# An RWKV-7 block and a SwiGLU block on one core: copies and scalings moved from VectorE to ScalarE, with a new order

## The chip, the cores and the metric

The kernel runs on one core of one Trainium2 chip. The time is the device time of one execution in microseconds (us), and the median of several runs counts. Each core has five engines that work side by side, each with its own queue that it takes in order: TensorE (PE in the profile, its weight loads PEld), VectorE (DVE), ScalarE (ACT), GpSimd (POOL) and SyncE (SP). SP and POOL here mostly issue DMA transfers.

## What is computed

Two blocks follow each other. The first is a recurrence over 768 time steps, for 4 batches of 8 heads with a head size of 40; its outputs are the tokens of the second, a feed-forward block over 3072 tokens of width 320 with 1536 hidden units.

```python
for t in range(S):
    y[:, :, t] = np.einsum('bhd,bhde->bhe', rt, state)
    Sa = np.einsum('bhde,bhe->bhd', state, at)
    state_decay = state * wt[:, :, None, :] - np.einsum('bhd,bhe->bhde', Sa, bt)
    state = state_decay + np.einsum('bhd,bhe->bhde', vt, kt)
...
rms = np.sqrt(np.mean(x * x, axis=-1, keepdims=True) + 1e-06)
xn = x / rms * rms_g
g = xn @ w_gate
silu = g * (1.0 / (1.0 + np.exp(-g)))
val = xn @ w_val
return (silu * val @ w_out).astype(np.float32)
```

The output at step t reads the state before that step's update, so the state that the last step leaves is read by nothing.

## The kernel before

The 768 steps are cut into 24 chunks of 32 (`NCH`, `C`). All 32 pairs of batch and head are worked on together: the 128 partitions hold two groups (`i`), two halves of the heads or of the factors (`o`, `q`), and the 32 steps of a chunk. All data is fp32.

Three stages make a chunk, and a fourth is shared by two chunks:

- `front(c)` loads w, a, k, b and v, transposes them on TensorE, and builds the products inside the chunk level by level (`LEVELS`: pairs of steps, then 4, 8, 16, 32). It leaves `LT`, the triangular matrices, `KN[l]`, the decayed k and b by level, with `KN[32]` for the whole chunk, `aP`, the decayed a, and `T[l]`, the products of the decays. `front` and `inverse` are written two chunks ahead of `main`.
- `inverse(c)` inverts the unit triangular matrices: 31 steps of two VectorE operations each (`tmp`, `Yi`), with transfers through DRAM (`sB`, `M`, `sY`) before and after to change the layout.
- `main(c)` is the recurrence proper. TensorE makes X from the incoming state and v, ScalarE negates it into `Xs`, TensorE makes U from it, and U is copied into `VU` beside v. From `VU` and `KN[32]` TensorE makes the state's update (kind `"update"`), and VectorE adds the decayed old state, `Sdec`, to it (`ST`). For the outputs, every second chunk loads and transposes the queries: `rE` holds them, and `r2` the same with the partition halves exchanged. Scores of queries against `VU` are masked into `As`, one part for each level, with the masks `msi`. The levels' products are summed into `y` (`down`). Last, tokens are transposed, normalized (`x`) and transposed again, and `xg` takes them times the norm's weights `gcol`, a column over partitions.
- `feed(g)` is the feed-forward block for the 256 tokens of two chunks. For each of 12 slices of 128 hidden units it loads weights (`wf`), makes gate and value products on TensorE (kinds `"h64"` and `"h"`), takes silu on ScalarE (`sg`), multiplies on VectorE (`hT`) and accumulates the output product in `po` (kind `"out"`). Before the first feed, `narrow` brings the float64 weights to fp32 and stores them in DRAM as `sW`; that is VectorE and ScalarE work (`ex`, `wf`, `o`).

Which engine does an operation is written in the helper's name: `tt`, `dcopy`, `ts` and `where` go to VectorE, `copy`, `act` and `scale` to ScalarE, `pe` to TensorE. `scale(o, a, by)` multiplies by a constant or by a column of one value for each partition.

The order of the work is written out by hand. Each helper call makes a piece in a list, with the pieces it depends on; `Plan.issue` then emits the pieces in the order of the string `ORDER`. A word of it says how far ahead of the first piece not yet emitted the next one stands; `-` emits a warm-up matmul into an unused part of `po` (L1000), which keeps TensorE busy in the first 230 us. `PAIRS` says which of three PSUM tiles each use of PSUM takes. Since all engines take their queues in order, this string fixes what stands before what on every engine. The functions that follow are the ones that the change touches; most profile lines name the helper (L475 VectorE, L502 and L505 ScalarE copies and scalings, L521 and L524 TensorE), so the tiles' names tell the operations apart.

Of the kernel before, what the change touches and what calls it, by code (L numbers as in the profile page):

```python
# [7 lines left out]
FP32 = mybir.dt.float32  # L8
# [8 lines left out]
P = 128  # L17
C = 32
LEVELS = (1, 2, 4, 8, 16)
CG = 2  # L20
WB = 5
S0, S1 = 15.0, 2.0
LEAD = 2
WARM = 230.0
# [21 lines left out]
36 33 2 26 42 1 31 0 25 343 37 29 107 38 24 36 26 34 262 2 13 1 35 40 0 190 24 339 13 14 - - - 40 17 44 15 41 43 55  # L46
42 8 60 47 175 72 48 45 84 185 59 68 186 585 54 58 - - - - - 49 93 586 53 179 69 71 599 81 176 57 597 50 67 178 609
70 188 80 622 51 92 16 623 65 610 52 56 177 633 64 66 - - - - - - - - - - - - 61 189 9 598 77 79 187 78 587 620 62 0
587 81 - - - - 72 75 179 82 62 90 595 384 194 588 87 11 633 89 589 74 395 620 197 590 380 88 73 195 391 - - - - 101
196 209 390 610 84 102 214 381 201 611 202 5 212 86 213 383 591 85 0 222 92 591 611 17 95 221 224 223 384 94 234 225  # L50
- - 197 233 237 93 391 245 246 592 328 393 198 598 645 612 0 641 598 15 612 592 - 338 205 206 380 642 599 209 0 207
612 200 0 337 612 186 598 6 326 613 2 599 641 34 176 200 216 217 23 600 389 215 33 201 355 95 202 177 96 214 - - - -
211 187 339 93 0 577 0 561 578 297 579 171 192 53 187 191 - - - 182 188 200 623 172 185 625 186 580 562 581 612 355
582 199 1065 197 583 611 183 198 624 184 0 152 1005 850 298 0 298 0 837 295 0 0 0 83 130 298 148 0 298 83 0 507 307
833 0 303 555 0 840 307 0 290 0 67 125 316 314 0 132 125 67 0 0 131 314 0 286 325 0 130 0 298 130 0 291 292 - - - -
- 287 0 293 0 304 0 316 305 301 0 0 283 0 296 0 311 0 322 281 0 286 0 295 280 0 292 - - - - - - - - - - - - - - - -
- 288 0 0 0 0 301 0 285 62 301 116 305 0 283 250 116 0 - - - - - - - - 293 0 258 112 296 0 110 300 256 0 308 307 245
293 292 0 0 304 0 288 0 301 - - - - - - 298 306 0 0 313 0 297 0 0 0 293 310 494 301 0 494 0 302 0 0 299 492 0 0 296
0 246 0 791 0 0 0 787 0 0 93 468 2 796 94 469 0 94 462 794 0 467 93 94 290 461 95 462 96 468 511 97 469 291 98 470
481 289 99 292 471 0 99 100 101 471 102 472 103 481 511 104 482 105 488 106 489 107 483 2 490 108 109 0 293 109 490  # L60
0 108 0 0 379 0 379 387 0 387 369 0 405 378 387 406 0 - - - - - - - - - - - - - - - - - - - - - - - - - - - - - - -
- - - - - - - - - - - - - - - - - - - - - - - - - - - - - - - - - - - - - - - - 44 0 367 377 0 415 0 42 0 414 383 43
412 0 383 410 0 383 40 373 0 0 0 0 0 0 36 0 377 - - - - - - - - - - - - - - - - - 44 0 377 35 44 0 414 0 0 82 0 32 -
43 0 373 0 90 0 229 407 38 88 0 40 78 226 42 38 41 47 48 0 43 226 42 50 45 48 396 0 50 396 43 0 396 0 0 379 395 380
0 395 380 0 401 0 394 0 378 242 400 44 0 400 47 0 145 45 377 242 0 145 391 377 0 216 1 145 391 42 635 398 429 626
146 0 397 39 145 426 634 398 146 147 631 43 623 44 621 45 632 46 148 47 622 - - - - 639 375 376 149 48 416 239 641
830 150 399 377 640 840 0 150 641 653 48 838 151 658 152 645 828 - - - - - - 642 153 670 154 646 155 682 49 656 50
156 669 657 51 157 666 158 667 52 159 643 668 - - - - - - - 53 389 160 161 678 162 1 651 652 - 647 2 702 655 3 654 0
594 610 611 609 625 595 636 109 608 110 596 373 - - - - - - - - - - - 605 590 374 111 345 783 607 626 782 383 112
627 620 622 385 793 113 623 606 375 382 114 792 621 - - - - - - - 617 384 115 376 346 116 377 619 117 635 634 118  # L70
618 378 119 - - - - - 160 633 120 379 121 163 380 161 122 381 123 162 124 164 386 - - - - - - - - - 629 125 387 126
127 128 388 129 630 130 640 631 389 638 131 390 - - - - - 167 641 132 391 133 639 134 392 168 135 393 - - - - - 165
136 394 137 138 430 139 166 571 431 581 643 140 - - - 171 721 644 580 141 642 142 570 143 174 645 144 173 145 178 -
- - 182 175 146 177 147 172 150 149 179 - - - 180 148 637 176 185 732 432 186 433 0 1065 584 283 - 39 1064 36 582 38
284 638 37 40 635 583 0 17 635 480 625 567 497 40 18 624 498 41 284 568 626 42 285 499 627 43 570 286 642 636 44 500
2 706 287 45 643 897 0 493 500 501 643 287 897 656 644 648 2 45 597 907 502 649 494 0 457 860 458 0 613 0 457 611
552 0 - 596 457 621 598 0 622 0 456 595 610 853 457 622 458 634 854 0 505 - - - 500 360 765 521 361 449 531 519 764
504 532 543 362 508 363 0 500 517 543 501 4 515 363 502 364 506 419 514 365 5 366 516 367 0 367 419 368 421 369 370
420 422 44 0 370 - 430 371 44 0 3 40 0 367 426 368 369 370 504 371 37 372 373 374 375 429 376 526 525 521 377 505
522 0 338 466 390 339 397 377 9 340 391 341 392 342 430 393 398 343 480 440 400 378 439 395 387 429 396 394 403 408  # L80
388 0 403 0 342 474 700 403 578 0 700 403 342 709 490 343 0 474 7 696 405 343 709 475 403 344 0 487 706 472 0 485
695 10 343 704 404 0 404 0 4 404 37 405 0 401 31 337 481 402 45 0 474 3 337 338 41 339 402 0 42 3 0 398 705 399 471
50 335 400 898 336 703 470 401 337 37 907 338 339 402 27 480 699 908 704 340 403 341 897 479 486 701 889 343 700 584
478 890 713 714 481 899 702 719 28 706 559 900 342 712 29 560 731 30 0 531 9 0 9 683 684 17 10 0 10 454 0 450 552 10
451 0 10 672 0 672 - - - - - - - - - - - - - - - - 662 25 0 27 670 26 0 682 680 24 695 539 677 676 678 704 661 37 -
- - - 3 36 675 662 296 4 681 434 691 663 679 692 703 672 5 0 0 428 1 680 683 42 682 666 43 687 681 667 20 40 686 21
677 695 2 22 292 0 675 705 287 0 675 287 688 0 671 0 669 665 269 7 17 410 8 682 29 411 412 30 667 413 414 0 8 665 0
675 8 681 672 9 674 0 9 672 - - - - - - - - - - 481 0 9 37 483 411 0 471 0 25 5 401 6 402 403 404 471 7 39 405 473 -
- - - - - - - - - - - 16 0 0 28 8 27 397 0 397 28 0 397 0 654 462 0 5 396 36 8 397 398 37 399 14 47 462 15 0 457 10
723 44 3 11 43 458 583 644 21 12 646 582 4 13 645 461 0 571 21 13 572 458 393 22 14 394 15 466 0 391 455 19 0 372 0  # L90
16 436 0 694 28 5 27 442 6 695 371 439 7 0 696 0 451 370 435 6 760 0 745 0 428 0 741 362 425 0 751 433 362 741 0 748
362 0 425 423 358 733 0 358 0 744 358 432 359 360 0 427 428 0 7 359 0 359 15 0 359 360 6 0 425 0 428 442 359 360 361
362 363 364 0 360 361 742 362 0 362 363 364 419 365 742 366 367 2 368 423 751 369 370 371 372 373 424 675 374 7 0
424 2 0 1154 672 0 1154 421 422 732 432 738 0 669 730 1002 732 670 420 995 731 439 742 685 985 421 0 993 421 687 735
422 686 743 4 1002 423 748 736 991 424 746 983 366 757 367 759 368 425 992 369 744 0 369 746 371 757 755 370 759 768
425 767 736 582 0 582 3 583 584 0 584 751 0 582 746 774 0 731 0 431 737 731 747 421 745 0 731 364 580 0 580 739 581
582 439 583 584 2 424 585 740 757 0 759 740 753 754 760 585 755 586 750 366 587 424 588 365 589 425 364 590 419 591
363 752 592 593 0 347 174 346 175 331 176 342 177 0 177 178 0 178 7 179 342 180 181 359 182 8 183 184 185 186 187
188 189 12 341 190 352 191 192 349 193 194 350 224 195 196 351 0 222 9 224 5 0 4 217 7 0 214 328 335 218 16 332 226
219 343 344 0 417 223 267 338 182 224 266 183 13 184 276 185 0 183 222 184 274 185 186 223 187 330 188 20 189 338 0  # L100
229 223 0 223 188 189 190 191 226 194 227 192 3 225 229 193 224 239 4 0 231 4 0 228 7 233 193 234 238 235 338 339
236 340 532 341 239 12 530 240 194 241 533 195 242 541 197 243 0 538 240 9 608 10 241 536 338 4 13 339 527 242 340
192 539 243 341 342 343 244 0 339 340 240 341 342 0 538 342 240 343 0 16 343 324 344 539 737 345 346 538 727 540 552
# [290 lines left out]
def kernel(  # L394
# [41 lines left out]
    N = 8  # L436
# [116 lines left out]
    for j, l in enumerate(LEVELS):  # L553
        nc.vector.tensor_scalar(iw[:, 2], iw[:, 0], j, None, ALU.logical_shift_right)
        nc.vector.tensor_scalar(msk[:, j], iw[:, 2], 1.0, None, ALU.is_equal)
# [477 lines left out]
```

## Time and profile before

| | us |
|---|---|
| median of 3 runs | 1108.51 |
| the runs | 1103.67 to 1111.27 |
| profiled execution, its own time | 1109.57 |
| its span, first to last instruction | 1107.8 |

The page cuts the span into 40 slices of 27.7 us. Each digit is the busy share in tenths, 9 being 90% or more; PEclk is the clock that TensorE was granted.

```profile
PE   5698889989999999999999999999999999999998
DVE  5999998899798889799789689988878889798421
ACT  4645554644235335325335335325325335332211
PEclk9799999989999999999999999999979999999999
```

The first eight slices or so are the start: front stages of the first chunks, weights brought to fp32, the first feed. The long middle repeats with every pair of chunks, and in the last slices only feeds are left. Busy time of a matmul is modelled from its start, so a full slice of PE is not a proof of peak rate.

The chain of waits that ended last, by engine:

```profile
PE 59%; DVE 26%; issue 4%; DMA 4%; ACT 4%; POOL 2%; SPq 1%; DVEq 0%; POOLq 0%; ACTq 0%
```

In these groups the first number is the count, then busy time in us and the mean of one in ns. They are the operations that the change takes from VectorE (the 128x512 group of `As` holds two masks for each chunk, those of level 16 and of level 1):

```profile
L475 DVE TENSOR_TENSOR As<-ps,msi 128x512 f32<-128x512 f32 x48 | 32.3, 682 | 8.0 <-PE ps L521 8.0
L475 DVE COPY VU<-ps 32x320 f32<-32x320 f32 x48 | 23.2, 483 | 3.0 <-PE ps L521 2.1
L475 DVE COPY r<-ps 64x512 f32<-64x512 f32 x24 | 16.5, 688 | 1.0 <-PE ps L524 0.4
L475 DVE TENSOR_TENSOR xg<-ps,gcol 128x384 f32<-128x384 f32 x24 | 13.5, 562 | 5.2 <-PE ps L524 5.1
```

### The profile page before, as it was taken

How to read it: one execution, taken by the hardware profiler on the slowest of the kernel's cores; microseconds unless marked ns; L12 is line 12 of the kernel's file. 1: busy time of each engine (PE TensorE's matmuls, PEld its weight loads, DVE VectorE, ACT ScalarE, POOL GpSimd, SP SyncE). 2: the span in 40 equal slices, each digit the busy share in tenths (PEclk: the TensorE clock that was granted, in tenths of full speed). 3: DMA queues.
4: the chain of work that ended last, by engine and by line, in shares of the span. 5: the costliest groups of instructions: out<-in, count | busy, mean ns of one | idle time of the engine just before them, and what ended most of it. 6: DMA issues, size and time to landing. Idle time of an engine off the chain costs nothing.

```text
span 1107.8 us, 53122 instructions
## 1 busy us (share of the span) xinstructions
PE 1043.1 (94%) x23152; PEld 862.2 (78%) x23152; DVE 906.1 (82%) x3065; ACT 453.9 (41%) x989; POOL 302.4 (27%) x534
## 2 busy tenths in 40 slices
PE   5698889989999999999999999999999999999998
PEld 5597777867878877877877887877878788888876
DVE  5999998899798889799789689988878889798421
ACT  4645554644235335325335335325325335332211
POOL 7621344022323422412422422422303412200000
PEclk9799999989999999999999999999979999999999
DMA  7635555675645645546535635635546536434242
GB/s 158 155 75 155 132 115 133 188 225 143 160 120 121 157 104 141 132 118 151 126 99 139 149 107 150 142 96 151 119 108 149 126 109 150 108 108 130 80 141 80
DMA packets 171177, 145.43 MB, mean 131 GB/s; under 512 B 123712, under 2 KB 142080, under 8 KB 170944
## 3 DMA queue, kind: packets, MB, share of 16 engines
q1 hardware_dynamic: 152576, 119.06, 39.7%
q0 software_dynamic: 16192, 22.64, 10.5%
q8 instruction: 182, 2.98, 1.2%
q10 hardware_dynamic: 2176, 0.33, 0.2%
q14 instruction: 51, 0.42, 0.1%
HBM read 125.83 MB, written 16.12 MB: 128 GB/s over the span
## 4 chain that ended last, share of the span: by engine, by line
PE 59%; DVE 26%; issue 4%; DMA 4%; ACT 4%; POOL 2%; SPq 1%; DVEq 0%; POOLq 0%; ACTq 0%
PE ps L521 40%; PE po L521 11%; PE ps L524 8%; DVE LT L475 4%; DVE tmp L475 3%; DVE Yi L475 3%; DVE K L475 2%; DVE As L475 2%; DVE ex L475 2%; DVE wf L475 2%; DVE y L475 1%; SPq L518 1%; DVE Ab L475 1%; ACT K L502 1%; DVE r L475 1%
## 5 line engine op out<-in xcount | busy, mean ns | idle before, releaser
L521 PE MATMUL ps<-xg,wf 128*128 128x256 f32 (+1 forms) x1728 | 357.6, 395 | 2.5 <-DVE xg L475 1.6
L521 PEld LDWEIGHTS ps<-xg,wf 128*128 128x128 f32 (+1 forms) x1728 | 263.1, 190 | 58.0 <-issue 15.2
L521 PE MATMUL po<-wf,hT 128*128 128x320 f32 x576 | 178.6, 444 | 2.7 <-DVE hT L475 1.3
L475 DVE TENSOR_TENSOR tmp<-Yi,M 128x60 f32<-128x60 f32 (+24 forms) x744 | 156.1, 210 | 19.2 <-DMA M<-sB 3.0
L475 DVE TENSOR_TENSOR Yi<-Yi,tmp 128x60 f32<-128x60 f32 (+24 forms) x744 | 155.4, 209 | 15.9
L498 ACT ACTIVATE sg<-ps 128x256 f32<-128x256 f32 x144 | 53.6, 382 | 239.9 <-PE ps L521 222.9
L518 POOL DMA_DIRECT2D VU<-in_v_dram x92 | 53.3, 586 | 354.0 <-PE ps L524 207.5
L521 PEld LDWEIGHTS po<-wf,hT 128*128 128x128 f32 x576 | 102.3, 190 | 38.8 <-issue 3.7
L475 DVE TENSOR_TENSOR hT<-ps,sg 128x256 f32<-128x256 f32 x144 | 59.3, 419 | 54.7 <-ACT sg L498 53.4
L521 PEld LDWEIGHTS ps<-Ab,K 40*64 40x64 f32 x4608 | 77.8, 139 | 30.5 <-issue 9.7
L475 DVE TENSOR_TENSOR K<-K,T 128x512 f32<-128x512 f32 (+1 forms) x192 | 93.5, 495 | 8.8 <-ACT K L502 3.0
L521 PE MATMUL ps<-Ab,K 40*64 40x56 f32 x4608 | 87.4, 226 | 11.2 <-DVE K L475 3.1
L502 ACT COPY K<-K 128x256 f32<-128x256 f32 (+1 forms) x168 | 71.3, 443 | 61.8 <-PE ps L521 38.5
L475 DVE TENSOR_TENSOR As<-ps,msi 128x256 f32<-128x256 f32 (+1 forms) x192 | 83.2, 481 | 13.1 <-PE ps L521 12.9
L502 ACT COPY KN<-ps 128x640 f32<-128x640 f32 x96 | 66.4, 692 | 54.8 <-PE ps L524 21.4
L521 PEld LDWEIGHTS ps<-As,KN 128*40 128x40 f32 x3072 | 67.2, 125 | 18.7 <-issue 10.7
L521 PE MATMUL ps<-As,KN 128*40 128x32 f32 x3072 | 74.5, 206 | 6.1 <-issue 3.4
L1000 PE MATMUL po<-ident 128*128 128x128 f32 x560 | 72.9, 284 | 5.3 <-ACT po L544 5.3
L518 POOL DMA_DIRECT2D kbn<-in_b_dram x92 | 53.8, 587 | 83.0 <-PE ps L521 72.3
L518 POOL DMA_DIRECT2D wn<-in_w_dram x92 | 51.5, 565 | 85.7 <-DVE tmp L475 32.5
L518 POOL DMA_DIRECT2D kbn<-in_k_dram x92 | 53.3, 583 | 75.0 <-PE ps L521 74.3
L1000 PEld LDWEIGHTS po<-ident 128*128 128x128 f32 x560 | 67.6, 197 | 6.7 <-POOL wan L514 5.2
(124 smaller groups left out, 1546.8 us busy)
## 6 DMA issues: line engine op xcount, KB each, us to landing
wf<-sW SPq DMA_DIRECT2D x144, 480.0 KB, 4.1
M<-sB SPq DMA_DIRECT2D x96, 128.0 KB, 3.7
rn<-in_r_dram SPq DMA_DIRECT2D x24, 160.0 KB, 4.3
sW<-ex SPq DMA_DIRECT2D x16, 240.0 KB, 3.0
out_dram<-o SPq DMA_DIRECT2D x48, 80.0 KB, 3.6
kbn<-in_b_dram POOLq DMA_DIRECT2D x92, 40.0 KB, 3.1
wan<-in_w_dram POOLq DMA_DIRECT2D x46, 80.0 KB, 4.2
wan<-in_a_dram POOLq DMA_DIRECT2D x46, 80.0 KB, 4.0
```

The lines of the kernel that those rows point to most:

```text
L475: plan.add("DVE", time + more + each * size(o), 0.087, lambda at: fn(at(o), *m(at)), [o], aps(*args))
L498: scalar(o, [a], lambda at: nc.scalar.activation(at(o), at(a), f, **kw), aps(acc), 0.1 if f in (AF.Square, AF.Relu) else 0.0)
L502: scalar(o, [a], lambda at: nc.scalar.copy(at(o), at(a)), extra=more)
L518: plan.add(by, 0.6 if by == "POOL" else 0.45, 0.0, lambda at: queue.dma_start(out=o, in_=i), [o], [i], load=LOADS[load], since=since)
L521: return o, lhsT, rhs, lambda at: nc.tensor.matmul(at(o), lhsT, rhs, start=start, stop=stop, skip_group_check=True), 4
L524: return o, i, ident, lambda at: nc.tensor.transpose(at(o), i, ident), 2
L1000: plan.warm = lambda: nc.tensor.matmul(po_[:, 0, DM:DM + P], ident, ident, start=False, stop=False, skip_group_check=True)
```

## The change

Five edits and a new order:

- U's four copies into `VU` are all made by ScalarE; two of them were on VectorE.
- The two copies that make `r2` go to ScalarE.
- The mask of level 16, which was one VectorE multiplication, becomes two ScalarE scalings by a column of `msi`, one for each group. At this level a mask is constant along the row, so a column says all of it.
- The multiplication by the norm's weights, which was one VectorE operation for three blocks of 128 tokens, becomes three ScalarE scalings by a column of `gcol`.
- The last chunk makes no new state: its `KN[32]` (eight transposes and a copy), `Sdec` and the update product are left out.
- `ORDER` and `PAIRS` are replaced as a whole.

There is also a way to invert and solve in two blocks of 16 steps, for chunks below `BLOCKS`. `BLOCKS` is 0, so none of it is emitted; it leaves behind one small constant, `lower`.

```diff
+BLOCKS = 0
...
+    lower = const.tile([P, 1], FP32, name="lower")
+    nc.vector.tensor_scalar(lower, msk[:, 4, 0:1], -1.0, None, MUL)
...
-        z["KN"][32] = KN_[32].next()
-        copy(z["KN"][32].rearrange("p (n o e) -> p n o e", n=N, o=2),
-             turned(K.rearrange("p (n i) x s -> p n (i x s)", i=2)).rearrange("p n (o e) -> p n o e", o=2)[:, :, :, 0:D])
+        if c + 1 < NCH:
+            z["KN"][32] = KN_[32].next()
+            copy(z["KN"][32].rearrange("p (n o e) -> p n o e", n=N, o=2),
+                 turned(K.rearrange("p (n i) x s -> p n (i x s)", i=2)).rearrange("p n (o e) -> p n o e", o=2)[:, :, :, 0:D])
...
-        if c > 0:
+        if 0 < c < NCH - 1:
             tt(Sdec, ST.rearrange("p n i d -> p (n i) d")[:, :, 0:D], z["T"][32].to_broadcast((P, NI, D)), MUL)
...
         for i, q in each_iq:
-            (copy, dcopy)[q](VU[other(i, 4 * q), 4 * q:4 * q + 4, :, 0:D].rearrange("p n o d -> p o n d"),
+            copy(VU[other(i, 4 * q), 4 * q:4 * q + 4, :, 0:D].rearrange("p n o d -> p o n d"),
                              U[other(i, 4 * q), :, 0:4 * D].rearrange("p o (n d) -> p o n d", n=4), more=0.09)
-        up = plan.room()
-        pe("update", [mm(up[part(o), i, col(slot(n))], kn(z, 32, i, n, o), VU[half(i), n, o, 0:D]) for n, i, o in each])
+        if c + 1 < NCH:
+            up = plan.room()
+            pe("update", [mm(up[part(o), i, col(slot(n))], kn(z, 32, i, n, o), VU[half(i), n, o, 0:D]) for n, i, o in each])
...
-            dcopy(R["r2"][half(0)], ps[half(1), :, 0])
-            dcopy(R["r2"][half(1)], ps[half(0), :, 1])
+            copy(R["r2"][half(0)], ps[half(1), :, 0])
+            copy(R["r2"][half(1)], ps[half(0), :, 1])
...
-            if G == 1 or l == 1:
-                tt(As[:, j], sc.rearrange("p o n t -> p (o n) t")[:, :, None, 1 if l == 1 else 16:C:2 if l == 1 else 1].to_broadcast((P, NI, 2, 16)),
+            if G == 1:
+                for i in range(2):
+                    scale(As[:, j, :, i], sc.rearrange("p o n t -> p (o n) t")[:, :, 16:C], msi[:, j, i, 0:1])
+            elif l == 1:
+                tt(As[:, j], sc.rearrange("p o n t -> p (o n) t")[:, :, None, 1:C:2].to_broadcast((P, NI, 2, 16)),
                    msi[:, j:j + 1].to_broadcast((P, NI, 2, 16)), MUL)
...
-        tt(xg[c // CG][:, :, c % CG * P:(c % CG + 1) * P], ps, gcol[:, :, None].to_broadcast((P, KT, P)), MUL)
+        for kt in range(KT):
+            scale(xg[c // CG][:, kt, c % CG * P:(c % CG + 1) * P], ps[:, kt], gcol[:, kt:kt + 1])
```

## The prediction

> **What bounds the kernel now.** I read the page's engine rows and slices first, then windows by stage, then what ended TensorE's waits, then one odd stretch in the timeline.
>
> ```profile
> PE 1043.1 (94%) x23152; PEld 862.2 (78%) x23152; DVE 906.1 (82%) x3065; ACT 453.9 (41%) x989; POOL 302.4 (27%) x534
> L1000 PE MATMUL po<-ident 128*128 128x128 f32 x560 | 72.9, 284 | 5.3 <-ACT po L544 5.3
> ```
>
> ```profile
> 0.00:80.00 80.00, 58.59 (x1118) 54.00 (x1119) 63.90 (x200) 41.95 (x84) 43.93 (x94) 0.89 0.57 128
> 80.00:240.00 160.00, 141.48 (x3465) 123.02 (x3463) 149.13 (x487) 85.73 (x167) 44.44 (x75) 0.98 0.59 159
> 240.00:1040.00 800.00, 780.64 (x18023) 637.31 (x18020) 677.83 (x2342) 317.16 (x717) 213.47 (x364) 0.99 0.51 129
> 1040.00:1108.00 68.00, 62.35 (x558) 47.85 (x557) 15.19 (x37) 9.11 (x24) 0.55 (x1) 1.00 0.32 98
> ```
>
> The first fence is the page's engine row and the warm-up group; the second is windows, with columns length, busy time of PE, PEld, DVE, ACT and POOL, granted clock, DMA share, GB/s. Two regimes: up to 240 us VectorE is busy 149.1 of 160 us (93%) and TensorE fills its gaps with warm-up matmuls (72.9 us of its 1043.1, the last at 219.7 us); from 240 to 1040 us TensorE is busy 780.6 of 800 (98%) and VectorE 85%. So TensorE's own work sets the time; the idle time that a lighter VectorE can remove is 18.5 us in 80 to 240 and 19.4 us in 240 to 1040. What ended those waits, from 240 us on:
>
> ```profile
> PE ps L521 <- issue: 4.3, 10, 0.9
> PE ps L521 <- DVE LT L475: 2.2, 3, 1.4
> PE ps L521 <- ACT KN L502: 1.6, 3, 0.8
> PE ps L521 <- DVE xg L475: 1.6, 2, 0.9
> PE po L521 <- DVE hT L475: 1.3, 3, 0.9
> ```
>
> Adding all rows of this answer (the smaller ones are not shown), VectorE ended 8.2 us of TensorE's waits and ScalarE 4.4. The same answer for 80 to 240 us has 18.1 us, 10.2 of them ended by VectorE.
>
> One stretch costs more than its idle time. TensorE paused near 811 us, and then ran at half clock:
>
> ```profile
> 810.00:815.00 5.00, 2.84 (x153) 2.40 (x156) 4.79 (x13) 1.66 (x4) 0.00 (x0) 0.89 0.35 102
> 815.00:820.00 5.00, 5.00 (x124) 4.53 (x116) 3.13 (x10) 2.31 (x4) 1.46 (x3) 0.50 0.05 9
> 820.00:825.00 5.00, 5.00 (x83) 3.86 (x76) 2.40 (x9) 0.69 (x1) 0.84 (x2) 0.50 0.41 69
> 825.00:830.00 5.00, 5.00 (x131) 4.01 (x130) 3.32 (x10) 0.38 (x1) 0.00 (x0) 0.74 0.47 117
> ```
>
> ```profile
> 809.39 2.23 DVE L475 COPY_PREDICATED LT<-near,ps 128x384 f32<-128x384 uint32 x3
> 811.65 0.49 DVE L475 COPY VU<-ps 32x320 f32<-32x320 f32 x1
> 811.68 1.16 PE L521 MATMUL ps<-Ab,K 40*64 40x56 f32 x64 [1.44 <-DVE LT L475]
> ...
> 812.40 0.48 DVE L475 COPY VU<-ps 32x320 f32<-32x320 f32 x1
> 813.02 0.82 PE L521 MATMUL ps<-VU,KN 64*40 64x40 f32 x64 [0.19 <-DVE tmp L475]
> ```
>
> The reader should see TensorE wait 1.44 us for 2.23 us of predicated copies, and VectorE's two U copies stuck behind them, so that the state update (ps<-VU,KN, 0.82 us), which could have filled the pause, comes after it. ScalarE's own two U copies ran from 809.09 for 0.85 us; with all four there the update would have been ready near 810.8. Clock lost: 0.11, 0.50, 0.50 and 0.26 of four 5 us windows, 6.9 us; with the 2.16 us of idle, 9.0 us for this hole. It is the only one between 300 and 1100 us.
>
> **The change part by part.** The counts in the built order confirm the edit: VectorE 3067 to 2947 instructions, ScalarE 975 to 1166, SyncE's queue 714 and GpSimd's 539 in both. BLOCKS is 0, so the block branches issue nothing. No DMA is added or dropped; all queues are re-laid by the new order, but with the same stagger: ahead of feed 0's last out product stand 2570 matmuls for 2572, 738 VectorE instructions for 758, 306 on ScalarE for 273, and ahead of its last weight load 210 entries of SyncE's queue for 209.
>
> VectorE loses 48 U copies at 483 ns (23.2 us), 24 r2 copies at 688 (16.5), 24 masks at 682 (16.4; the 128x512 row has 48, half of them level 16), 24 xg scalings at 562 (13.5) and one Sdec (0.8): 70.4 us, 906 to 836. It gains one 128x1 setup instruction, near the 166 ns of the 128x16 row.
>
> ScalarE gains 48 U copies at 417 ns (20.0, its own row), 24 r2 copies near 593 (14.2, the 128x512 copy from PSUM), 48 masks and 72 xg scalings by a column. A column operand costs 95 ns here (x<-ps,ss 530 ns against Xs<-ps 435, both 128x320). A mask is the 371 ns of y<-ps 128x256 plus 95, 466 ns, 22.4 us; an xg piece the 272 ns of the single po<-ps 128x128 copy plus 95, 367 ns, 26.4 us. Less one KN copy (0.7): +82.3 us, 454 to 536, 48% of the span.
>
> [...] the exchange is a loss of about 12 us of engine time (82.3 for 70.4), more if latency counts: per chunk the mask grows by 2 x 466 - 682 = 250 ns, xg by 3 x 367 - 562 = 540, the U copies from two beside two to four in a row, 0.70 us; 1.5 us x 24 = 36 us if all of it were on the path. The rows weigh more: ScalarE stood idle 217.6 us from 240 us on just for silu's product from TensorE, and TensorE has other chunks' matmuls to run meanwhile. I price it at +1, ends 0 and +36: today's 4.4 us of waits ended by ScalarE, scaled by 536/454, is +0.8. If the cover failed, late silu would delay hT and TensorE's out products.
>
> TensorE's own work: the last chunk drops 8 transposes (26.4 us / 24 = 1.1) and 32 update products (20.4 / 24 = 0.85); two warm-up words fewer are four instructions of 72.9/560 us, 0.5. In 1000 to 1040 us TensorE is busy 40.00 of 40, so nothing hides these: -2.5.
>
> Start: 8 U copies, 4 r2, 4 masks and 3 xg lie before 240 us, 3.9 + 2.8 + 2.7 + 1.6 = 11.0 us of VectorE. Upper end 10.2 (all waits that VectorE ended), lower end 0: 278 of 280 warm-up words stay in TensorE's queue and take their time even where the gap they were laid for has closed, and chains through ScalarE and DMAs stay. I take -4, nearer the lower end for that reason.
>
> Steady part: VectorE falls from 85% to about 78%. Of the 8.2 us of waits, 1.6 belong to the hole at 811; of the other 6.6 I take -3, ends 0 and -6.6. What is late next is PSUM and TensorE itself.
>
> The hole: U copies no longer stand behind predicated copies on VectorE. All of it gone is -9.0; another order may have one elsewhere. I take -4. [...] The trace shows 0.50 after a window with 2.16 us of scattered idle, so short holes do cost clock here; the measurement decides.
>
> Sum: -2.5 - 4 - 3 - 4 + 1 = -12.5 on a span of 1107.8, so 1095.3, and with the 1.8 us around it (1109.57 - 1107.8) 1097.1. The profiled run stands 1.1 above the median of 1108.5: 1096.
>
> **The rivals.**
>
> No gain beyond TensorE's own work: it is 98% busy, its waits are short, and what VectorE no longer delays is delayed by PSUM turnover or warm-up matmuls. For: VectorE itself waits 52.3 us for silu before hT and 22.2 us for TensorE before y from 240 us on. Against: the DVE rows above. 1108.5 - 2.5 = 1106.
>
> Full relief: -2.5 - 10.2 - 6.6 - 9.0 = -28.3, 1080. For: VectorE busy 93% from 80 to 240 us, so the start is bound by it. Against: warm-up matmuls stay, and chains have other members.
>
> Slower: ScalarE's queue makes holes. It runs in order, and in the new order 16 of the 144 silus stand directly behind a mask scaling that waits for the score product; a silu held up holds hT and then the out products. A hole like the one at 811 costs 9.0 us, most of it clock. The saving of 12.5 is eaten at the second; from the third on the kernel is slower by over 1%: 27 - 12.5 = +14.5, 1123. For: the half clock exists and 120 new pieces (48 masks, 72 xg) wait on fresh PSUM results. Against: only one such hole in 800 us today, and silus wait for TensorE, not the reverse.
>
> **How the numbers follow.** The forecast 0.55, no gain 0.15, full relief 0.12, slower 0.18. One per cent of 1108.5 is 11 us, about what a measurement of this kernel can tell from no change (the three runs spread over 7.6): faster means under 1097.4. The forecast's own spread, 1086 to 1105, lies 0.58 below that: faster 0.55 x 0.58 + 0.12 = 0.44, same 0.55 x 0.42 + nearly all of 0.15 = 0.37, slower 0.19. The range 1082 to 1117 leaves out about half of full relief and two thirds of slower, some 0.19.
>
> **What would show it.** Right: VectorE near 836 us and ScalarE near 536; xg pieces near 367 ns and masks near 466; TensorE's busy time near 1040; waits ended by VectorE from 240 us on under 6 us; no half-clock window after 300 us. Wrong: waits of po on hT or of hT on sg grown by more than a few us, two or more half-clock windows, or warm-up matmuls ending later than 219.7 us.

## The result, and the profile after

| | before | after |
|---|---|---|
| median, us | 1107.91 (4 runs, 1103.67 to 1111.27) | 1124.28 (4 runs, 1121.78 to 1129.1) |
| ratio to before, 95% interval | | 1.0124 (1.0084 to 1.0164) |
| span of the profiled execution, us | 1107.8 | 1121.4 |

The changed kernel is slower by 1.2%, where 1.1% less was forecast. First the page's engine row of the changed kernel, and two of its windows (length, then busy time of PE, PEld, DVE, ACT and POOL, granted clock, DMA share, GB/s):

```profile
PE 1042.5 (93%) x23076; PEld 857.6 (76%) x23076; DVE 850.0 (76%) x2945; ACT 518.5 (46%) x1180; POOL 302.5 (27%) x534
```

```profile
80.00:240.00 160.00, 136.92 (x3349) 117.79 (x3347) 137.65 (x448) 91.25 (x189) 39.61 (x68) 0.97 0.57 149
240.00:1040.00 800.00, 770.24 (x17821) 626.38 (x17821) 632.67 (x2251) 367.05 (x860) 217.54 (x371) 0.99 0.51 129
```

VectorE was relieved as meant: 149.1 us of 160 became 137.7 in the start, 677.8 became 632.7 in the middle. But TensorE, which was to fill up, is busy less in both: 141.5 to 136.9 and 780.6 to 770.2. The moved operations cost what was worked out for them:

```profile
L505 ACT COPY VU<-ps 32x320 f32<-32x320 f32 x96 | 40.0, 417 | 12.8 <-PE ps L524 9.9 <-DVE Yi L478 1.4
L508 ACT ACTIVATE xg<-ps,gcol 128x128 f32<-128x128 f32 x72 | 22.0, 369 | 12.4 <-PE ps L527 12.1
L508 ACT ACTIVATE As<-ps,msi 128x256 f32<-128x256 f32 x48 | 20.5, 472 | 39.9 <-DVE As L478 28.8 <-PE ps L524 4.6 <-DVE tmp L478 3.4
L505 ACT COPY r<-ps 64x512 f32<-64x512 f32 x24 | 13.9, 580 | 8.3 <-PE ps L527 8.0
```

What ended TensorE's waits from 240 us on, changed kernel (us in total, times, longest); before, the first row was 4.3 us in 10 times:

```profile
PE ps L524 <- issue: 15.3, 20, 2.4
PE po L524 <- DVE hT L478: 2.6, 4, 1.7
PE ps L524 <- ACT KN L505: 2.2, 4, 1.0
PE ps L524 <- DVE LT L478: 1.8, 4, 0.7
PE ps L524 <- DVE As L478: 1.8, 1, 1.8
```

One row has grown, and it has no releaser: "issue" means that TensorE waited for nothing that the profile shows. Counted over the whole trace, with all waits above 0.1 us after TensorE's first instruction:

| profiled execution, us | before | after |
|---|---|---|
| TensorE's waits put down to "issue" | 8.7 (15 times) | 26.2 (33 times) |
| all its other waits | 45.0 | 41.4 |
| its busy time, without overlaps | 1043.1 | 1042.5 |

The differences sum to +17.5 - 3.6 - 0.6 = +13.3; the span grew by 13.6. So the question is what these waits are. Near 749.7 us one of them stands inside a run of small products, between two of the same kind (timeline of the changed kernel: start, length, operation, count, wait before it):

```profile
745.69 1.13 PE L524 MATMUL ps<-rE,vut 40*64 40x32 f32 x64
...
749.75 0.28 PE L524 MATMUL ps<-r,Sd 40*40 40x32 f32 x2 [2.41 <-issue]
```

No data can be late there: the products before it in the run read the same tiles. The chain of waits that ended last runs through it (start, length, what):

```profile
745.69 1.65 PE ps L524 x113
747.34 2.41 issue
749.75 3.77 PE ps L524 x19
```

Summed over the trace, 22.5 of the 26.2 us lie on this chain; before, 6.2 of the 8.7 did.

Two things tell where these waits come from. Counted in matmuls, the waits of before lie on a grid: with one period of 127.12 matmuls all 15 fall on the same phase. In the changed kernel 29 of the 33, with 24.1 of the 26.2 us, fall on the same phase of the same period. A matmul here is two instructions, itself and its weight load (the page counts 23076 of each), so this is one period of 254.2 of them. And the queue table of the page has a row for transfers of instructions (number, MB, share of the DMA engines' time); first before, then changed:

```profile
q8 instruction: 182, 2.98, 1.2%
q8 instruction: 181, 2.97, 1.1%
```

Each of these transfers moved 16 KB (2.98 MB by 182, 2.97 by 181); in the changed kernel 2 x 23076 instructions by 181 are 255 to a transfer. All 15 "issue" waits of before, and the same 29 of the 33 of the changed kernel, end 1.2 to 1.6 us after such a transfer has landed. Theory A, an inference from these counts: TensorE's instructions come in blocks of one such period, some 255, and when a block is used up in less time than the next one needs to come, TensorE waits. A group of 64 recorded small products (1.16 us in the timeline of before at 811.68) is then half a block, and a wide product of 16 recorded matmuls (3.72 us in `e4` below) an eighth of one. So two groups of small products in a row empty a block in about 2.3 us.

### The profile page after: what moved, and what is told of

It is laid out like the page before. It is cut to its first block, busy times and chain, and to the rows that moved or that the text cites. A ratio compares the mean times of both kernels' runs of the same rounds, so it can differ in the third digit from the quotient of the medians.

```text
span 1121.4 us, 53033 instructions
## 1 busy us (share of the span) xinstructions
PE 1042.5 (93%) x23076; PEld 857.6 (76%) x23076; DVE 850.0 (76%) x2945; ACT 518.5 (46%) x1180; POOL 302.5 (27%) x534
## 3 DMA queue, kind: packets, MB, share of 16 engines
q8 instruction: 181, 2.97, 1.1%
## 4 chain that ended last, share of the span: by engine, by line
PE 68%; DVE 15%; issue 6%; ACT 6%; DMA 4%; SPq 1%; POOL 1%; DVEq 0%; POOLq 0%; ACTq 0%
PE ps L524 45%; PE po L524 13%; PE ps L527 9%; DVE LT L478 2%; DVE tmp L478 2%; DVE Yi L478 2%; DVE K L478 2%; PE po L1039 1%; DVE ex L478 1%; DVE y L478 1%; DVE wf L478 1%; ACT K L505 1%; DMA LT<-sY 1%; ACT KN L505 1%; DVE Ab L478 1%
## 5 line engine op out<-in xcount | busy, mean ns | idle before, releaser
L478 DVE TENSOR_TENSOR Yi<-Yi,tmp 128x60 f32<-128x60 f32 (+24 forms) x744 | 156.7, 211 | 17.5 <-DVE tmp L478 0.4
L521 POOL DMA_DIRECT2D VU<-in_v_dram x92 | 53.1, 584 | 356.3 <-PE ps L527 214.0
L524 PEld LDWEIGHTS ps<-Ab,K 40*64 40x64 f32 x4608 | 75.1, 134 | 33.3 <-issue 14.9
L524 PE MATMUL ps<-Ab,K 40*64 40x56 f32 x4608 | 85.2, 221 | 13.6 <-issue 4.2
L478 DVE TENSOR_TENSOR As<-ps,msi 128x256 f32<-128x256 f32 (+1 forms) x168 | 68.6, 456 | 18.7 <-PE ps L524 15.0
L524 PEld LDWEIGHTS ps<-As,KN 128*40 128x40 f32 x3072 | 66.1, 124 | 17.2 <-issue 12.5
L521 POOL DMA_DIRECT2D kbn<-in_b_dram x92 | 54.2, 592 | 85.4 <-PE ps L524 76.0
L521 POOL DMA_DIRECT2D kbn<-in_k_dram x92 | 53.3, 583 | 82.6 <-PE ps L524 80.4
L521 POOL DMA_DIRECT2D wn<-in_w_dram x92 | 51.5, 566 | 84.5 <-DVE KN L478 34.6
```

The lines of the kernel that those rows point to most:

```text
L478: plan.add("DVE", time + more + each * size(o), 0.087, lambda at: fn(at(o), *m(at)), [o], aps(*args))
L521: plan.add(by, 0.6 if by == "POOL" else 0.45, 0.0, lambda at: queue.dma_start(out=o, in_=i), [o], [i], load=LOADS[load], since=since)
L524: return o, lhsT, rhs, lambda at: nc.tensor.matmul(at(o), lhsT, rhs, start=start, stop=stop, skip_group_check=True), 4
```

## The experiments

In this part, kernels that keep the old order have the moved pieces at the places of those that they replace. "Issue", other waits and busy time are of the profiled execution, counted as above; medians are of 4 to 22 runs (`e4` ran once), and each ratio is to the kernel before beside it on the same chip. The runs of one kernel spread over 2 to 17 us, so a few us in a column that comes from one execution mean little. All these kernels carry the unused block code with its constant `lower`.

### Which part of the change costs: order and edits apart

`e1_all_old_order` is the changed kernel with the old `ORDER` and `PAIRS`; `e2_none_new_order` has the new ones, and the four moves taken back (U, `r2`, mask, `xg`).

```diff
 # e1: ORDER, PAIRS of before, all edits
 # e2: ORDER, PAIRS of after, and
-            copy(VU[other(i, 4 * q), ...
+            (copy, dcopy)[q](VU[other(i, 4 * q), ...
...
-        for kt in range(KT):
-            scale(xg[c // CG][:, kt, ...
+        tt(xg[c // CG][:, :, ...
```

> All five edits, but in the order of before: each moved piece stands where the piece it replaces stood, and PSUM turns are as before. Theory A (the new order lays TensorE's small products so close together that its instructions are not fetched in time; 26 us of stalls inside groups of products against 9 before): the stalls are back near 9 us and the time is below before, 1096 to 1106. Theory B (ScalarE's longer queue delays the products): nothing of that goes away, since ScalarE has the same work; 1116 to 1126.

> The new order with the four moves undone: U copies, query copies, the mask of level 16 and the norm's weights are on VectorE again, at the places that the order gives them; the last chunk still makes no state. Theory A: TensorE's sequence is the slow one, so stalls stay near 26 us and the time is 1120 to 1135 (VectorE heavier again). Theory B: ScalarE is relieved, 1106 to 1112.

`e3_copies_old_order` moves only the copies of U and `r2`; with the last chunk's cut it is `e5`. `e6` moves only the mask, `e7` only `xg`, each in the old order. `e8` is the changed kernel with mask and `xg` back on VectorE.

```diff
 # e3 and e5, against before
-            (copy, dcopy)[q](VU[other(i, 4 * q), ...
+            copy(VU[other(i, 4 * q), ...
...
-            dcopy(R["r2"][half(0)], ps[half(1), :, 0])
+            copy(R["r2"][half(0)], ps[half(1), :, 0])
```

> The order of before, and only the U copies and the query copies moved to ScalarE. Theory A: 1102 to 1109, stalls near 9 us. Theory B, if these moves are the ones that hurt: 1114 or more.

> The order of before, the U and query copies on ScalarE, and no state from the last chunk; masks and the norm's weights stay on VectorE. The copies alone gave 0.9967 of before. The last chunk's missing products are 2.0 us of TensorE work near the end with nothing beside them, so 1102 to 1107, ratio 0.994 to 0.997, below before and after both. If the last chunk's cut costs something in the old order (an idle stretch where its products stood), the ratio is 0.998 or more.

> The order of before, and only the mask of level 16 moved, as two ScalarE scalings. All five edits in the old order gave 1.0056, the copies 0.9967; the two scalings must make up some 0.9% between them. Theory B1 (TensorE waits for the norm's weights: 6.9 us of its waits ended by xg there): the mask is near harmless, 0.998 to 1.003. Theory B2 (the masks hold VectorE's other masks, 21.4 us of waits there): 1.004 or more.

> The order of before, and only the norm's weights moved, as three ScalarE scalings. Theory B1: 1.005 to 1.010, with 6 us or more of TensorE's waits ended by xg. Theory B2: 0.998 to 1.003.

> The new order with the copies on ScalarE and no state from the last chunk, but mask and norm's weights back on VectorE at the places that the order gives them. If the order is slow for its TensorE sequence alone (theory A), the stalls inside groups of products stay near 24 us and the time is 1118 to 1130. If the scalings on ScalarE are what makes the changed kernel slow, 1104 to 1112.

| kernel | order | median, us | ratio (95%) | issue | other waits |
|---|---|---|---|---|---|
| e3, copies | old | 1106.99 | 0.9967 (0.9946 to 0.9988) | 10.2 | 41.2 |
| e5, copies, last chunk | old | 1105.49 | 0.9971 (0.9955 to 0.9987) | 10.2 | 43.0 |
| e6, mask | old | 1112.78 | 1.0046 (1.0030 to 1.0062) | 8.7 | 47.3 |
| e7, xg | old | 1114.20 | 1.0058 (1.0039 to 1.0077) | 9.4 | 44.4 |
| e1, all edits | old | 1115.82 | 1.0056 (1.0023 to 1.0088) | 9.9 | 48.8 |
| e8, copies, last chunk | new | 1120.82 | 1.0129 (1.0087 to 1.0171) | 21.1 | 41.5 |
| after, all edits | new | 1124.28 | 1.0124 (1.0084 to 1.0164) | 26.2 | 41.4 |
| e2, last chunk | new | 1148.72 | 1.0347 (1.0304 to 1.0391) | 22.6 | 58.9 |

In the old order the copies gain 0.3%, the last chunk nothing that can be told, and the two scalings lose about 0.5% each, so that both theories on them (`e6`, `e7`) were half right. All edits together lose 0.6% with "issue" at 9.9 us: the changed work by itself is slower in the order of before. In `e1` Theory A had the waits right and the time wrong (1096 to 1106 expected); 1115.82 lies at the edge of Theory B's 1116 to 1126, and ScalarE's scalings are indeed what delays there. `e7` shows how a scaling costs time: TensorE now waits for the three scalings, 1.1 us in a row, where it waited 1.6 us in all for the one multiplication (PE's waits, whole run):

```profile
PE ps L524 <- ACT xg L508: 6.4, 11, 1.2
```

In `e6` it is the other masks on VectorE that wait behind ScalarE's two (DVE's waits):

```profile
DVE As L477 <- ACT As L507: 22.3, 21, 4.0
```

In the new order no cost of the same scalings can be told (1.0124 with them, 1.0129 without, each within 0.4%). The order is what costs there: `e5` and `e8` have the same code except for `ORDER` and `PAIRS`, and are 0.9971 and 1.0129. That is 15 us between their medians; "issue" rose by 10.9 us and the other waits fell by 1.5. Every kernel in the new order has 21 to 26 us of "issue" waits, every one in the old order 9 to 10. And without the moves the new order is the worst of all, beyond the 1120 to 1135 that Theory A gave for `e2`: its "issue" waits are 22.6 us, as expected, but its other waits are 17.5 us more than the changed kernel's. `PAIRS` was never changed apart from `ORDER`.

### Does a dense run by itself show it

`e4_run_of_small` is the kernel before with work added behind its output: 40 groups of 32 small products back to back, then 40 such groups with 8 wide products between each two.

```diff
+        for rep in range(40):
+            small()
+        wide(64)
+        for rep in range(40):
+            small()
+            wide(8)
```

> Before, with products added after its last output products, which feed nothing: first 40 groups of 32 small products (64x56, as in the front stage) back to back, then 40 such groups with 8 wide products (128x256) after each. No transfers but the last outputs run then. Theory A: in the first part TensorE is held to one fetch of instructions per 3.3 us or so, that is 1.65 us for each group in the mean, with gaps inside groups, once what was fetched ahead is used up; in the second part a group takes the 1.16 us that it takes elsewhere, with no gaps. Theory B, or gaps that come from transfers: 1.1 to 1.2 us for each group in both parts.

First the dense part in its timeline, then the part with wide products between:

```profile
1109.92 2.13 PE L1048 MATMUL ps<-A,K 40*64 40x56 f32 x128 [1.34 <-issue]
1113.68 14.38 PE L1048 MATMUL ps<-A,K 40*64 40x56 f32 x512 [1.63 <-issue]
1128.40 7.43 PE L1048 MATMUL ps<-A,K 40*64 40x56 f32 x256 [0.35 <-issue]
1136.18 3.68 PE L1048 MATMUL ps<-A,K 40*64 40x56 f32 x128 [0.35 <-issue]
...
1209.66 1.16 PE L1048 MATMUL ps<-A,K 40*64 40x56 f32 x64
1210.74 3.72 PE L1053 MATMUL ps<-xg,wf 128*128 128x256 f32 x16
1214.39 1.16 PE L1048 MATMUL ps<-A,K 40*64 40x56 f32 x64
```

The waits come at multiples of 128 matmuls, with their weight loads 256 instructions, which is taken as the block from here on; there are none once wide products stand between. Where the clock was still full (1.00 from 1100 to 1110 us, 0.59 in the mean of the next 10 us) a block of 2.13 us was followed by a wait of 1.63. Then the clock fell to half (0.50 from 1120 to 1180 us), and a block alone took 3.6 to 3.7 us, followed by a wait of up to 0.35. From 1113.68 to 1174.74 us 16 blocks took 61.06 us, 3.8 each, for 2.13 + 1.63 = 3.76 at full clock. That is the price in this run: its small products back to back went through a block in 3.8 us in the mean at either clock, and where the work of a block took less, a wait made up the rest. A group took 1.9 us where 1.65 were expected, because a block took 3.8 us and not 3.3, the estimate that went into the expectation; the 1.16 us of the second part came as expected.

### Moving the ends of the blocks

The sharpest test leaves all real work in its order: a warm-up word is four instructions (two matmuls, 560 for before's 280 words, and their weight loads), so leaving out 32 of before's 280 moves every later end of a block by half a block, and 64 by a whole one, which brings the ends back to the same work. They were taken out evenly, every eighth or ninth, or every fourth or fifth.

```diff
 # e9: ORDER, the first of 32
-... 177 633 64 66 - - - - - - - - - - - - 61 189 ...
+... 177 633 64 66 - - - - - - - - - - 61 189 ...
```

> The kernel before with 32 of the 280 warm-up words left out, every eighth or ninth, nothing else (8.3 us less of filler on TensorE). Its stalls that nothing in the profile explains come at every 256th instruction of TensorE, and the points sit where few of the dense runs of small products fall; leaving out 32 words (128 instructions) moves every later point by half a block. Theory A (TensorE's instruction supply, and where the blocks end): from the trace of before, with at least 3.3 us for a block, the shortfall rises from 8 us to about 24 us with this shift, so issue-ended waits go from 8.7 us to 20 to 30 us, and the time to +8 to +18 us. Rival B (the waits are another effect of the order itself, as full PSUM rooms or semaphores that the profile does not show): the waits stay where they were in the work, 8 to 10 us, and the time within 3 us of before. Rival C (fillers matter: less of them lets the clock fall at the start): a granted clock under 0.95 in 80 to 240 us and no change after.

> The same with 64 of the 280 words left out (256 instructions): the points come back to where they were in the work, one block later. Theory A: issue-ended waits near those of before, 7 to 13 us, and a time within 4 us of before, although more filler is gone than with 32. Rival C (fillers): twice the loss of the shift by half a block. Rival B: as before.

> The changed kernel with 32 of its 278 warm-up words left out. Its own points are already near the best place by the same count (shortfall 9.8 us of 8 to 29), so Theory A: the waits grow from 26 us to 35 to 50 us and the time by 5 to 18 us over the changed kernel, to 1129 to 1142. Rival B: the same waits and the same time as the changed kernel, 1124 within 4.

> The changed kernel with 64 of its 278 warm-up words left out, which moves the ends of the blocks by one whole block. Theory A: issue-ended waits 22 to 32 us, near the changed kernel's 26, not the 36 of the shift by half a block, and 1120 to 1130 us. Rival C (fillers matter in the new order): slower than the shift by half a block, above 1150 us.

| kernel | median, us | ratio (95%) | issue | other waits | busy |
|---|---|---|---|---|---|
| before | 1109.71 | | 8.7 | 45.0 | 1043.1 |
| e9, before, half a block | 1155.41 | 1.0424 (1.0380 to 1.0467) | 34.6 | 48.3 | 1060.1 |
| e10, before, a whole block | 1111.24 | 1.0022 (1.0002 to 1.0042) | 13.1 | 54.6 | 1027.9 |
| after | 1124.28 | 1.0124 (1.0084 to 1.0164) | 26.2 | 41.4 | 1042.5 |
| e11, after, half a block | 1150.06 | 1.0351 (1.0325 to 1.0378) | 36.0 | 49.5 | 1051.8 |
| e14, after, a whole block | 1120.02 | 1.0095 (1.0063 to 1.0128) | 22.0 | 50.1 | 1034.8 |

Eight us less work made the kernel before 46 us slower; twice the cut brought it back to within 1.5 us (15 us less busy time, and 14 us more waits). No theory of fillers or of the order's dependences says that, so these waits are the ends of blocks, and they set time. The clock granted from 80 to 240 us did fall with fewer fillers, from 0.98 to 0.95 in `e9`; but `e10`, with fewer still, has before's mean of 0.981 over the whole span. For the changed kernel half a block cost more than was expected (1150 for 1129 to 1142 us), a whole one no more than expected.

The table says something on the change itself, too. Where the ends lie as built, or a whole block later, the changed kernel is the slower one (1.0124, and 1.0095 for 1.0022). With half a block left out of both, on the same chip, it is the faster one: 1150.06 for 1155.41 us. So at a size of one per cent even the sign of the change hangs on where the blocks end; these are two places of many.

The same run of products in `e9` and in before shows one of these waits (timelines; the first is `e9`):

```profile
372.05 1.15 PE L522 MATMUL ps<-Ab,K 40*64 40x56 f32 x64
373.02 0.81 PE L522 MATMUL ps<-VU,KN 64*40 64x40 f32 x63
...
373.64 1.08 PE L522 MATMUL ps<-rE,vut 40*64 40x32 f32 x58
377.73 0.31 PE L522 MATMUL ps<-rE,vut 40*64 40x32 f32 x5 [3.01 <-issue]
```

```profile
362.42 0.81 PE L521 MATMUL ps<-VU,KN 64*40 64x40 f32 x63
...
363.05 1.13 PE L521 MATMUL ps<-rE,vut 40*64 40x32 f32 x63
364.11 1.34 PE L521 MATMUL po<-wf,hT 128*128 128x320 f32 x4
```

Counted back 128 matmuls from the wait, the block in `e9` begins near 372.9 us and is empty 1.8 us later, five products before the end of the group; in before an end falls elsewhere and the group runs through. The loss is more than the waits. By spans (1154.0 - 1107.8 = 46.2): waits +25.9, other waits +3.3, and busy time +17.0 although 8.3 us of fillers are gone (64 matmuls by 72.9/560 us). That leaves 25 us for a slower clock, and the mean granted clock says nearly the same: 0.963 of 1154.0 us, which is 43 us lost, for 0.981 of 1107.8 before, 21 us. Two windows of `e9` after the wait of 3.01 us show it granted 0.88 and 0.78:

```profile
375.00:380.00 5.00, 2.27 (x12) 1.64 (x13) 2.93 (x8) 0.00 (x0) 1.10 (x2) 0.88 0.42 70
380.00:385.00 5.00, 5.00 (x37) 3.71 (x37) 4.48 (x21) 0.85 (x2) 0.00 (x0) 0.78 0.79 201
```

My count from the trace of before, a shortfall of 24 us with an estimated 3.3 us for a block, was too low for `e9`: a block took 3.8 in `e4`, and the clock was not in it at all.

### Repairing the new order

`e12_new_order_spread` issues ten wide products of the changed kernel earlier, so that each lies in a block that ended in one of ten of the waits; `e13_new_order_spread_near` puts the same ten as late in the block as it can. `e15_copies_last_spread` does it in `e5`, with four.

```diff
 # e12, one of ten: ORDER, a product of feed 6 (8 recorded matmuls) ahead of main's query products
+feed 6: ps<-xg,wf
 main: ps<-rE,Sd and ps<-r,Sd
...
-feed 6: ps<-xg,wf
```

> The changed kernel with ten wide products (nine gate or value products or the like of 16 matmuls or 8, and output products) issued 35 to 98 matmuls earlier, so that each falls into the block of 256 instructions that ended in one of ten of the unexplained waits (753, 257, 382, 2253, 352, 2406, 1207, 274, 292 and 389 ns, 8.6 us in all); no block ends elsewhere in the work by more than that, nothing else changes. Theory A: most of these ten waits are gone, issue-ended waits 26 to about 17 to 20 us, and the time 5 to 10 us under the changed kernel, 1114 to 1119. Rival B: the waits stay, the time within 3 us of the changed kernel.

> The same ten wide products as in the spread repair, in the same blocks, but put as late as their block allows, so that most are moved by less (8 to 66 matmuls ahead of the block's end for 35 to 98). Theory A with lost cover (what came back as other waits, 7.9 us, came because the products left the places where they covered waits): issue-ended waits again 14 to 19 us, the other waits 42 to 46 us instead of 49.3, and 1113 to 1119 us. Rival D (the repaired waits were not on the critical path: the chain of chunks sets the time in the new order): 1120 to 1125 us again, with other waits near 49.

> The old order with the copies on ScalarE and no state from the last chunk (1105.5 us), with four wide products put into blocks that ended in waits of 291, 224, 757 and 991 ns. Theory A: 1 to 2 us less waits of this kind and 1 to 3 us less time, which can hardly be told from none: 1102.5 to 1105.5 us. Lost cover or rival D: the same time or slower by up to 3 us.

The stretch that was shown of the changed kernel at 745 us, now in `e12`: the wait of 2.41 us is one of 0.16.

```profile
746.61 1.14 PE L524 MATMUL ps<-rE,vut 40*64 40x32 f32 x64
747.67 1.99 PE L524 MATMUL ps<-xg,wf 128*128 128x256 f32 x8
...
750.40 0.23 PE L524 MATMUL ps<-r,Sd 40*40 40x32 f32 x2 [0.16 <-issue]
```

| kernel | median, us | ratio (95%) | issue | other waits |
|---|---|---|---|---|
| after | 1124.28 | 1.0124 (1.0084 to 1.0164) | 26.2 | 41.4 |
| e12, ten moved, far | 1122.71 | 1.0104 (1.0070 to 1.0139) | 16.0 | 49.2 |
| e13, ten moved, near | 1123.65 | 1.0153 (1.0112 to 1.0193) | 17.6 | 46.6 |
| e15, e5 with four moved | 1108.17 | 0.9984 (0.9964 to 1.0003) | 10.2 | 50.8 |

The waits could be taken away where the theory said, 10.2 and 8.6 us of them, and the time did not follow: 7.8 and 5.2 us came back as waits for other things (for `hT` 3.9 us became 6.1 and 4.5, for `KN` 2.2 became 3.7 and 4.0), and the medians cannot be told from the changed kernel's. The expectation of 5 to 10 us failed. On the chain that ended last 9.0 us of "issue" were left in `e12`, for 22.5, so the chain runs through other work instead. Whether the products are missed where they came from, or the chain of chunks would have been late in any case and only stood hidden behind the waits, these runs don't tell: moving the products less far (`e13`) gave back a third less, and no time. In `e15` the repaired waits are gone (291, 224 and 757 ns, and 991) but others of the same sum came elsewhere; it is no better than `e5`.

## Why the prediction was wrong

Two steps failed, each by more than the 12.5 us of gain that was summed up.

The first is a term put at nothing, the order. The prediction says that all queues are re-laid "but with the same stagger" and gives the new order no cost. It shows "PE ps L521 <- issue: 4.3, 10, 0.9" as the largest row of TensorE's waits, and then adds only what VectorE and ScalarE ended. With the copies moved and the last chunk cut, the order alone took the ratio from 0.9971 to 1.0129 (`e5`, `e8`), 15 us; "issue" made 10.9 of the 12.0 us by which the span of their profiled executions grew. From before to changed it rose by 11.0 us in the row shown and by 17.5 us in the whole trace.

The second is the size of the terms. In the order of before, where "issue" stayed at 9.9 us, the same edits lost 0.6% instead of gaining 1.1% (`e1`). ScalarE's scalings, put at +1, cost some 5 us (mask, `e6`) and 6 us (`xg`, `e7`) there: the waits that ScalarE ended from 240 us on were 11.0 us in `e1`, where 4.4 scaled by 536/454 had given 5.2. The moved copies, more than half of VectorE's relief, brought about 4 us (`e3`). The two steps do not add up: in the new order no cost of the scalings can be told.

Term by term:

- TensorE's own work, -2.5: the cut is there (23152 to 23076 matmuls), but the gain was not measured: `e5` with it and `e3` without it have 0.9971 and 0.9967, each within 0.2%, which is the size of the term.
- Start, -4: the waits of 80 to 240 us that VectorE ended fell from 10.0 (the rows' sum, which the prediction has as 10.2) to 8.2 us, half of the term; in the same stretch "issue" rose from 3.0 to 9.9. U's last copy of chunk 1 began at 127.9 us for 133.1 before, but that of chunk 3 at 222.3 for 219.8. In the old order (`e1`) the waits that VectorE ended there did fall to 4.1 us.
- Steady part, -3: waits ended by VectorE from 240 us on went from 8.2 to 9.0. VectorE's 45 us less work between 240 and 1040 us shortened none of TensorE's waiting. "What is late next is PSUM and TensorE itself" named the right engine and the wrong cause.
- The hole, -4: it is gone, as the term had it (window 815 to 825 of the changed kernel: clock 1.00). But the clock lost from 240 us on, summed over windows of 5 us, is 8.6 us for 8.8: a longer dip near 240 us and three short ones, two of them (625 and 750 us) right after "issue" waits of 1.0 and 2.4 us. The rival "slower" had asked for holes like that, and put them into ScalarE's queue.
- ScalarE, +1: waits ended by ScalarE from 240 us on went from 4.4 to 5.5, as the term had it, in the new order alone. In the old order the moved multiplications lost about 0.5% each (`e6`, `e7`), and no loss can be told in the new one (`e8`).
- The durations (369 ns for 367, 472 for 466, 580 for 593) and the engine time that they add up to were right: the durations of ScalarE's instructions sum to 82.7 us more, for 82.3. The page's busy rows move less, +64.6 and -56.1, because they count overlaps once. VectorE's durations sum to 66.9 us less, for 70.4; the prediction took such differences of durations from the busy rows ("VectorE near 836", "ScalarE near 536").

The slower rival had the sign and nearly the size, 1123, and that is luck. It asked for three or more holes of 9 us behind ScalarE's queue; after 300 us the one dip that came after waits ended by ScalarE (at 430 us: 0.7 us for `x`, 0.5 us for a moved copy into `r`) was 3.41 us of half clock. What stays open is how much of the +1.2% the block ends cause. The sum of the waits puts all of it on them, and moving them changes the time by 2 to 4%, but taking ten of them away in the new order gave nothing that can be measured. The version that beats both kernels, by 0.3%, is `e5` (or `e3`, which can't be told from it): the copies moved, the scalings left on VectorE, the old order kept.

## What to carry to other kernels

A wait that the profile can't explain may be a resource that the profile doesn't name: look whether its places have a period in instructions before leaving it out of a sum. Small products back to back took 3.8 us for every 256 of TensorE's instructions in `e4`; an estimate from that one run is that a stretch of this kernel with less than about 4 us of work in 256 may end in such a wait. With wide products between them `e4` had none, but in the changed kernel this was not shown to save time: moving ten of them (`e12`) took 10.2 us of the waits away and no time. Dropping instructions ahead moved the later ends of blocks: 128 of them were worth 4% in `e9`, which is more than any edit of the change. So time two kernels with their block ends at more than one place before a difference of a per cent is put down to an edit. And price a new order as a change of its own: run the edits in the old one first.

## What was not expected of the hardware

- In the traces of before and of the changed kernel, an instruction transfer of 16 KB took 1.05 us in the median. Counted from the first matmul of a block of the waits' grid, it started after 1.36 us (before) and 1.43 us (changed) in the median, and the waits on the grid ended 1.46 and 1.43 us in the median after it had landed. These add up to 3.9 us, about as long as a block of `e4` took.
- In a dense run of small products TensorE was busy 56.64 of 60 us and was granted half its clock all that time; with wide products between, it had the full clock. Whether the products' size or the waits of 0.35 us between blocks hold it down was not tested (windows of `e4`):

```profile
1120.00:1180.00 60.00, 56.64 (x1998) 54.37 (x1992) 0.00 (x0) 0.00 (x0) 0.00 (x0) 0.50 0.02 4
1190.00:1390.00 200.00, 200.00 (x3156) 168.71 (x3158) 0.00 (x0) 0.00 (x0) 0.00 (x0) 1.00 0.01 2
```

- The granted clock fell after windows of 3.41 us in which TensorE did little. In the traces of before and of the changed kernel the clock is full or half, and each of the 28 stretches between two changes is a whole number of 3.41 us, from 1 to 167. I cut both traces into windows of that length, in step with the changes, from 80 us to the last whole one. Each of the 10 falls to half clock follows a window in which TensorE was busy for 25 to 69%. Of the windows at full clock, those busy for less than 40% were all followed by a fall (4 of 4); from 50 to 60% it was 2 of 7, from 60 to 70% 3 of 13, above 70% none of 562. So in these traces it counted how much of a pause fell into one window, and none of the ten was idle altogether. In the changed kernel the wait of 2.41 us shown above fell into one window, and 3.41 us at half clock followed:

```profile
746.12:749.53 3.41, 1.22 (x99) 1.11 (x92) 1.91 (x9) 0.00 (x0) 1.69 (x3) 1.00 0.87 259
749.53:752.94 3.41, 3.19 (x21) 2.59 (x21) 2.25 (x6) 0.37 (x1) 0.00 (x0) 0.50 0.31 52
```

Near 811 us `e3` and `e5` have the same order. In `e3` the idle time was spread over three windows and the clock stayed full; in `e5` one window had 1.79 us of work in 3.41, and four windows at half clock followed, of which the first is shown. First `e3`, then `e5`:

```profile
804.02:807.43 3.41, 1.96 (x56) 1.29 (x60) 2.95 (x8) 1.67 (x5) 0.00 (x0) 1.00 0.42 112
807.43:810.85 3.42, 2.74 (x162) 2.55 (x153) 2.90 (x7) 2.00 (x6) 0.00 (x0) 1.00 0.19 72
810.85:814.26 3.41, 2.67 (x77) 1.93 (x74) 3.14 (x13) 2.48 (x4) 2.30 (x4) 1.00 0.21 37
```

```profile
809.93:813.35 3.42, 1.79 (x128) 1.67 (x128) 2.52 (x9) 1.31 (x5) 0.00 (x0) 1.00 0.51 149
813.35:816.76 3.41, 3.40 (x71) 3.30 (x72) 2.52 (x7) 1.28 (x3) 0.00 (x0) 0.50 0.00 0
```
